# A transformer block on one core: exponentials seven steps behind instead of eight, the last steps in pairs of banks

## The chip, the cores and the metric

The kernel runs on one core of a Trainium2 chip. The metric is the device time of one execution in microseconds (us). The core has five engines with a queue each: PE (TensorE, matmuls), DVE (VectorE), ACT (ScalarE), POOL (GpSimd) and SP (which issues the DMAs). Each engine works through its own queue in order and waits there for semaphores. Matmuls write to PSUM, which has eight banks of 128 x 512 float32; SBUF holds the rest.

## The reference

The input is one sequence of 2048 tokens with 512 features in bfloat16. The block has 32 heads of 16 features and a feed-forward part with 1792 hidden features.

```python
def _A_ref(x, wqkv, wo):                 # H = 32, Dh = 16
    qkv = (x @ wqkv).reshape(B, S, 3, H, Dh).transpose(2, 0, 3, 1, 4)
    q, k, v = qkv[0], qkv[1], qkv[2]
    p = softmax(einsum("bhqd,bhkd->bhqk", q, k) * Dh ** -0.5)
    o = einsum("bhqk,bhkd->bhqd", p, v)
    return o.transpose(0, 2, 1, 3).reshape(B, S, D) @ wo

def _B_ref(x, w_gate, w_up, w_down):
    return (gelu(x @ w_gate) * (x @ w_up)) @ w_down

h = x + _A_ref(layernorm(x), A_wqkv, A_wo)
out = h + _B_ref(layernorm(h), B_w_gate, B_w_up, B_w_down)
```

## The kernel before

**The work and its order.** Attention is cut into 64 units: eight groups of 256 query tokens (`gi`, the last is `GL` = 7) times eight slots of four heads (`slot`). Each unit takes 16 steps of one Python loop, the tick; a tick's instructions are put into the engines' queues one after the other when the program is built. The scores of a unit are computed twice. The first pass (P1, line 797 on PE) writes a pair of score tiles to two PSUM banks and DVE takes the row maximum over both (line 806). One such maximum is a tick of the loop; there are 1024. After a unit's last tick `negm_pre` (lines 832 to 840 on POOL) makes the negated maximum, `negm_post` turns it with a DMA transpose into `STG`, and four ticks later (`ADDX`) POOL adds it into the queries (line 851). The second pass (P2, line 867 on PE) then gives the scores less their maximum, transposed, and ACT takes the exponential of each bank of 128 x 512 (line 879) into a ring of 34 tiles: 23 in `PTM`, 4 in `PTE`, 7 in `PTG`. P2 runs `LAGX` = 8 ticks behind the end of its unit's P1 (`P2_START = 16 + LAGX`), two tiles a tick. So a tick of the main loop holds one maximum and two exponentials, and when P1 is over, 24 ticks of P2 alone remain.

**The dense stream.** All other PE work runs beside this as items, one piece a tick, from two lists, `prio` and `ready` (class `Dense`): the projections, `item_pv` (probabilities times values, line 893, five ticks for a unit), `item_ofin` (turning its result, line 919), `item_oproj`, and for each group the feed-forward part: seven steps `f` of `item_gate` and `item_up` (line 1072) and two `item_down` (line 1122, residual at 1127). An item of `ready` starts only if `startable` allows it and if it is over before the next item of `prio` is due. Before the change both `item_down` of group 6 (`GL - 1`) are held back until the loop is over (`force`) and serve as filler then. Results leave PSUM through `evac_act`: on ACT, and on DVE once P1 is over (`dve_free`). Where a tick's items have too little for PE, `dummy` adds matmuls (line 1285); in the ticks after P1 a pair of ticks is filled to `FILL_2`.

**POOL.** POOL's smaller chains (`PoolStream`) are a first-in-first-out list, emitted against a budget of 1.19 us a tick: the gelu of a feed-forward step (lines 1062, 1063, 1064, then tanh on ACT at line 1055, then 1060, 1061 and the product at 1114), and the end of `item_ofin`: the inverse of the row sums (`inv`, line 928) and the product (`mul`, line 932). An entry that costs over 2 us, which is `inv` alone, isn't emitted in ticks 1, 2, 3, 13, 14 and 15 of each 16.

**The end.** `tail_a` and `tail_a2` project three quarters of the last group's attention output inside the loop, into banks 0 and 1 (lines 1153, 1164, 1168). After the last `item_pv`, `tail_b` does the last slot (`tail_norm`, line 1192; `tail_onT`, 1205; projection, 1237), the layer norm (1240 to 1251, with one POOL operation at 1249), the transposes of the result (`tail_hnT`, lines 1213, 1218, 1220) and the last group's feed-forward part. Between the steps of this serial chain `fill(n)` puts `n` units of dense work or dummy matmuls on PE.

Of the kernel before, what the change touches and what calls it, by code (L numbers as in the profile page):

```python
# [223 lines left out]
LAGX = 8  # L224
PAUSE = 1
DOUBLES = 20
FILL_2 = 4
FILL_LN = 16
# [5 lines left out]
def bass_sequential_preLN__mha_block__geglu_ffn__prompt_kernel(nc, A_x, A_wqkv, A_wo, B_x, B_w_gate, B_w_up, B_w_down, out):  # L234
    dbg = None
    with ExitStack() as es:
# [264 lines left out]
        def startable(it, room):  # L501
            if it[0] is item_gate and par_busy[it[1][1] % 2] and room < 10:
                return False
            if it[0] is item_down and it[1][0] == GL - 1 and not force[0]:
                return False
            if it[0] is item_down and it[1][1] == 0 and not force[0]:
                return not gut_left.get(it[1][0], 0) and dense.now >= gut_last.get(it[1][0], 0) + 1
            return it[0] is not item_projT or not (qks_busy.get(("a", qk_n[0] % 4)) or qks_busy.get(("b", qk_n[0] % 2)))

        class Dense:  # L510
# [17 lines left out]
            def _start(self, item):  # L528
                genfn, a, est, nb = item
                if self.single:  # L530
# [5 lines left out]
            def piece(self):  # L536
                if self.single and self.pause > 0:
                    return 0
                while True:
# [11 lines left out]
                    try:  # L551
# [11 lines left out]
                        if self.single:  # L563
                            banks.give(self.bank)
                            self.pause = PAUSE
# [28 lines left out]
        class PoolStream:  # L594
# [11 lines left out]
            def run(self, flush=False):  # L606
                while self.q and (flush or self.budget >= min(self.q[0][0], 1.0)):
                    if not flush and self.q[0][0] > 2.0 and dense.now % 16 in (1, 2, 3, 13, 14, 15):
                        break
# [8 lines left out]
        ticking = [False]  # L618
        pool = PoolStream()
# [158 lines left out]
        for fn_ in qk_late:  # L778
            fn_()
        early = {0: [lambda: stats_dve(12), c2_rest], 1: [lambda: stats_dve(13), lambda: stats_dve(14), lambda: stats_act(15)], 2: [c2_dve, c3_rest],  # L780
                 5: [c3_act], 9: [lambda: w_order("q", 1, "act")], 11: [lambda: w_order("k", 1, "act")], 16: [lambda: w_order("q", 2, "act")],
                 18: [lambda: w_order("k", 2, "act")], 20: [lambda: w_order("q", 3, "act")], 22: [lambda: w_order("k", 3, "act")]}
# [59 lines left out]
        def negm_post(ui):  # L842
# [5 lines left out]
            q_ap = QT[:, c, slot, 256 * hf:256 * hf + 256]  # L848
            def add():
                pool.spend(0.7)  # L850
# [9 lines left out]
        def p2_tile(ui, j, gp, jj):  # L860
# [3 lines left out]
            m, g, b = j // 2, 2 * gp + jj, banks.take()  # L864
# [5 lines left out]
            return (b, m, g)  # L870

# [173 lines left out]
        def gelu_chain(par, dE):  # L1045
# [4 lines left out]
            def later(n):  # L1050
                if not force[0] and act_lag[0] > LAG_OP + 0.1 * n:
# [14 lines left out]
        def gate_up_mms(b, gi, f, w, nm):  # L1066
            hT = hnT_l[gi % 2]
            hr = [("hnT", gi % 2, k) for k in range(2)]
# [78 lines left out]
        def tail_a(b):  # L1147
# [9 lines left out]
            dense.add(tail_a2, front=True, est=4, not_before=dense.now + 2)  # L1157
            return 1

        def tail_a2(b):  # L1160
            gp = GL % 2
            for k in range(2):
                for hc in range(3):
                    P.op("pe", lambda e, k=k, hc=hc: e.matmul(pbank[:, k, :], OnT[:, k, hc, :], wo_sb[:, hc, :], start=(hc == 0), stop=False),
                         reads=[("OHa", 0), "wo"], writes=[("pb", k)], sig=False)
                    if hc == 1:
                        yield 2
                P.op("pe", lambda e, k=k: e.matmul(pbank[:, k, :], ident[:], g_h(GL, k), start=False, stop=False),
                     reads=["ident", ("h", gp, k)], writes=[("pb", k)], sig=(k == 1))
                if k == 0:  # L1170
                    yield 2
            a_done[0] = True
            return 2
        a_done = [False]
# [34 lines left out]
        def tail_hnT(b, k):  # L1209
            gp = GL % 2  # L1210
            pt = pbank[:, b, :].bitcast(BF16)
            for dc in range(4):
                P.op("pe", lambda e, dc=dc: e.transpose(out=pt[:, 128 * dc:128 * dc + 128], in_=hn_sb[:, k, 128 * dc:128 * dc + 128], identity=ident[:]),
                     reads=[("OH", k), "ident"], writes=[("pb", b)], sig=(dc == 3))
            o_ap = hnT_l[gp][:, :, 128 * k:128 * k + 128]
            i_ap = pt[:, 0:512].rearrange("p (c s) -> p c s", c=4)
            if k == 1:
                P.op("act", lambda e: e.activation(out=o_ap, in_=i_ap, func=ACT.Copy), reads=[("pb", b)], writes=[("hnT", gp, k)])
            else:
                P.op("dve", lambda e: e.tensor_copy(out=o_ap, in_=i_ap), reads=[("pb", b)], writes=[("hnT", gp, k)])  # L1220
# [6 lines left out]
        def tail_b():  # L1227
            P.op("act", lambda e: e.activation(out=htmp[:, 0:1], in_=nhalf[:, 0:1], func=ACT.Gelu_apprx_tanh), reads=["nhalf"], writes=[("htmp", 0)])
            fill(3)
            while not a_done[0]:  # L1230
                fill(1)
            in_bank(tail_norm)
            fill(3)
# [20 lines left out]
            for k in (0, 1):  # L1254
                in_bank(tail_hnT, k)
            fill(2)
# [6 lines left out]
            for k in range(2):  # L1263
                down_h(k, GL, k)
# [28 lines left out]
        while True:  # L1293
# [5 lines left out]
            if tick == P2_START - 4:  # L1299
# [23 lines left out]
            elif p2_ok and tick % 2 == 0:  # L1323
                if tick == 16 * NU:
                    for b_ in (2, 3):
                        banks.give(b_)
                for d_ in (0, 1):
                    for jj in (0, 1):
                        t2l.append(p2_tile((t2 + d_) // 16, (t2 + d_) % 16, 1 - (tick + d_) % 2, jj))
                        p2_consume((t2 + d_) // 16, t2l)  # L1330
                        t2l = []
# [75 lines left out]
```

## Time and profile before

| | |
|---|---|
| median of 3 runs | 1243.05 us (1242.91 to 1243.18) |
| the profiled execution's own time | 1243.15 us |
| its span, first to last instruction | 1241.4 us |
| granted TensorE clock, mean | 0.997 |
| DVE busy | 1189.8 us (96%), of it 1162.4 us in line 806 |
| ACT busy | 1199.9 us (97%) |
| PE busy | 1137.8 us (92%) |
| POOL busy | 764.3 us (62%) |

The span leaves out 1.75 us of the execution's time. Busy times are sums over the whole span; the last maximum of P1 ends at 1184.9 us, so the 56.5 us behind it have another limit than the loop ahead of it, and the shares of the whole say little about them. An ACT instruction's duration covers its latency; back to back, instructions overlap, so the distance from start to start is its price in a queue. Times in this document are us from the span's start unless said otherwise.

### The profile page before, as it was taken

The numbers are of one execution on the slowest core, as the hardware profiler recorded it, in microseconds if no ns is written. First come the engines' busy times: TensorE is split into PE (matmuls) and PEld (weight loads), VectorE is DVE, ScalarE is ACT, GpSimd is POOL, SyncE is SP. The second block draws the span as 40 slices with busy tenths as digits, with TensorE's granted clock in tenths as the row PEclk, the third lists the DMA queues.
The fourth block names the chain that finished last, engine by engine and source line by source line (L and its number), as shares of the span: only waits on it lengthen the run. The fifth ranks groups of instructions, "written<-read, shape, count | busy, mean of one in ns | idle before, by whom it ended". The sixth has DMA issues, their size and how long they took to land.

```text
span 1241.4 us, 31438 instructions
## 1 busy us (share of the span) xinstructions
PE 1137.8 (92%) x12680; PEld 437.8 (35%) x12680; DVE 1189.8 (96%) x1088; ACT 1199.9 (97%) x2464; POOL 764.3 (62%) x1540
## 2 busy tenths in 40 slices
PE   7999888899999999999999998999999999999998
PEld 3333222233333333333333333333333333333335
DVE  8999999999999999999999999999999999999923
ACT  7899999999999999999999999999999999999992
POOL 8647774467746765376645777367654766547760
PEclk9999999999999999999999999999999999999989
DMA  5101004300010000100010000100002000100000
GB/s 151 31 22 28 24 19 130 89 6 3 6 31 12 6 6 6 38 5 6 4 27 18 4 6 6 27 17 6 6 4 40 6 4 6 27 19 3 6 13 18
DMA packets 50800, 27.45 MB, mean 22 GB/s; under 512 B 36064, under 2 KB 49632, under 8 KB 50656
## 3 DMA queue, kind: packets, MB, share of 16 engines
q1 hardware_dynamic: 50656, 25.45, 8.0%
q8 instruction: 101, 1.65, 0.5%
q14 instruction: 43, 0.35, 0.1%
HBM read 11.80 MB, written 2.10 MB: 11 GB/s over the span
## 4 chain that ended last, share of the span: by engine, by line
DVE 58%; ACT 30%; PE 9%; POOL 2%; issue 1%; DMA 0%
DVE PM L806 57%; ACT PTM L879 17%; ACT PTG L879 5%; ACT PTE L879 3%; PE pbank L1122 2%; PE pbank L867 2%; PE pbank L797 1%; ACT th_sb L1055 1%; PE pbank L1072 1%; ACT g_sb L641 1%; ACT OnT L1012 1%; ACT u_sb L641 1%; PE pbank L739 1%; PE pbank L998 1%; PE pbank L676 1%
## 5 line engine op out<-in xcount | busy, mean ns | idle before, releaser
L806 DVE TENSOR_REDUCE PM<-pbank 128x2 f32<-128x1024 f32 x1024 | 1162.4, 1224 | 5.3 <-PE pbank L867 2.8
L879 ACT ACTIVATE PTM<-pbank 128x512 bf16<-128x512 f32 x1388 | 737.0, 669 | 4.7
L867 PE MATMUL pbank<-QT,KT 32*128 32x256 bf16 x4096 | 498.2, 273 | 9.7 <-ACT PTM L879 4.4
L797 PE MATMUL pbank<-KT,QT 32*128 32x512 bf16 x2048 | 394.2, 382 | 46.4 <-DVE PM L806 23.6
L1285 PE MATMUL pbank<-ones_bf,ident 128*128 128x512 bf16 x794 | 245.3, 384 | 28.1 <-ACT PTM L879 3.2
L797 PEld LDWEIGHTS pbank<-KT,QT 32*128 32x128 bf16 x2048 | 104.5, 91 | 392.7 <-DVE PM L806 170.3
L879 ACT ACTIVATE PTG<-pbank 128x512 bf16<-128x512 f32 x420 | 228.2, 660 | 1.1 <-PE pbank L867 0.3
L867 PEld LDWEIGHTS pbank<-QT,KT 32*128 32x128 bf16 x4096 | 164.5, 92 | 65.7 <-ACT PTM L879 36.8
L879 ACT ACTIVATE PTE<-pbank 128x512 bf16<-128x512 f32 x240 | 137.7, 667 | 1.9 <-PE pbank L867 1.1
L893 PE MATMUL pbank<-PTM,VA 128*17 128x256 bf16 x2776 | 125.8, 274 | 2.7 <-ACT PTM L879 1.2
L832 POOL TENSOR_TENSOR MX<-PM,MX 128x8 f32<-128x8 f32 x64 | 12.9, 202 | 163.9 <-DVE PM L806 163.9
L1285 PEld LDWEIGHTS pbank<-ones_bf,ident 128*128 128x128 bf16 x794 | 47.6, 97 | 131.4 <-ACT PTM L879 83.8
L928 POOL TENSOR_TENSOR LINV<-OAT,negone 128x16 f32<-128x16 f32 (+1 forms) x32 | 92.7, 2896 | 0.0
L893 PEld LDWEIGHTS pbank<-PTM,VA 128*17 128x17 bf16 x2776 | 60.1, 89 | 46.9 <-issue 29.1
L821 POOL TENSOR_TENSOR MX<-PM,MX 128x8 f32<-128x8 f32 x64 | 13.0, 203 | 101.5 <-DVE PM L806 101.5
L1072 PE MATMUL pbank<-hnT_l,wu_sb 128*128 128x256 bf16 x448 | 67.1, 276 | 3.1 <-ACT PTM L879 0.2
L1072 PE MATMUL pbank<-hnT_l,wg_sb 128*128 128x256 bf16 x448 | 66.9, 275 | 2.5
L1114 POOL TENSOR_TENSOR GUT<-th_sb,u_sb 128x512 bf16<-128x512 f32 x49 | 62.2, 1270 | 5.1 <-DVE u_sb L630 3.0
L1061 POOL TENSOR_TENSOR th_sb<-th_sb,g_sb 128x512 f32<-128x512 f32 x49 | 62.1, 1268 | 4.1
L1064 POOL TENSOR_TENSOR th_sb<-th_sb,g_sb 128x512 f32<-128x512 f32 x49 | 62.1, 1268 | 3.1
L1062 POOL TENSOR_TENSOR th_sb<-g_sb 128x512 f32<-128x512 f32 x49 | 51.0, 1041 | 18.8 <-ACT g_sb L641 18.8
L1122 PE MATMUL pbank<-wd_sb,GUT 128*128 128x512 bf16 x224 | 60.5, 382 | 0.6 <-ACT PTM L879 0.2
(149 smaller groups left out, 1077.3 us busy)
## 6 DMA issues: line engine op xcount, KB each, us to landing
QKS<-QKS SPq DMA_DIRECT2D x27, 112.0 KB, 2.2
x_sb<-in_A_x_dram SPq DMA_DIRECT2D x4, 512.0 KB, 5.6
xres<-in_A_x_dram SPq DMA_DIRECT2D x16, 128.0 KB, 2.2
out_dram<-out_sb SPq DMA_DIRECT2D x16, 128.0 KB, 1.8
wg_sb<-in_B_w_gate_dram SPq DMA_DIRECT2D x4, 448.0 KB, 5.0
wu_sb<-in_B_w_up_dram SPq DMA_DIRECT2D x4, 448.0 KB, 4.0
wd_sb<-in_B_w_down_dram SPq DMA_DIRECT2D x3, 512.0 KB, 6.4
STG<-ST SPq DMA_TRANSPOSE x64, 2.3
```

The costliest lines, as they stand in the source:

```text
L797: P.op("pe", lambda e, g=g, b=b: e.matmul(pbank[:, b, :], QT[32 * g:32 * g + 32, c, slot, 128 * qt:128 * qt + 128], KT[32 * g:32 * g + 32, ...
L806: P.op("dve", lambda e: e.tensor_reduce(out=PM[:, par, qt, kc, g:g + 2], in_=pbank[:, b:b + 2, :], axis=AX.X, op=ALU.max), reads=[("pb", b ...
L867: P.op("pe", lambda e, kt=kt, i=i: e.matmul(pbank[:, b, 256 * i:256 * i + 256], KT[32 * g:32 * g + 32, slot, 128 * kt:128 * kt + 128], QT[ ...
L879: P.op("act", lambda e, b=b, pi=pi: e.activation(out=PTt(pi), in_=pbank[:, b, :], func=ACT.Exp), reads=[("pb", b)], writes=[("PT", pi)], e ...
L893: P.op("pe", lambda e, g=g, kt=kt, pi=pi, i=i: e.matmul(pbank[32 * g:32 * g + 17, b, 0:256], VA[:, kt, 4 * slot + g, :], PTt(pi)[:, 256 * ...
L928: P.op("pool", lambda e: e.tensor_tensor(out=li, in0=oat4[:, :, :, 16], in1=negone[:, 0:8 * ns].rearrange("p (q h) -> p q h", q=2), op=ALU ...
L1061: o(1.27, lambda e: e.tensor_tensor(out=ts_, in0=ts_, in1=gs, op=ALU.mult), [("th", par), ("g", par)])], then=done)
L1064: o(1.27, lambda e: e.tensor_tensor(out=ts_, in0=ts_, in1=gs, op=ALU.mult), [("th", par), ("g", par)])], then=lambda: defer(TANH_LAG, lamb ...
L1072: P.op("pe", lambda e, dc=dc, fc=fc, i=i: e.matmul(pbank[:, b, 256 * i:256 * i + 256], w[:, dc, 128 * fc:128 * fc + 128], hT[:, dc, :], st ...
L1114: P.op("pool", lambda e: e.tensor_tensor(out=o_ap, in0=shp(ts_), in1=shp(us), op=ALU.mult), reads=[("th", par), ("u", par)], writes=o_keys ...
L1122: P.op("pe", lambda e: e.matmul(pbank[:, b, :], GUT[:, fc, 128 * k:128 * k + 128], wd_sb[:, fc, :], start=first, stop=last), reads=[("GUT" ...
L1285: P.op("pe", lambda e: e.matmul(pbank[:, b, :], ident[:], ones_bf[:, 0:512], start=True, stop=True), reads=["ident", "ones_bf"], writes=[( ...
```

## The change

- `LAGX` goes from 8 to 7: P2 runs one tick nearer behind P1, so 23 ticks are left after P1. The loop's switch to one dense item at a time stays at tick 20 (`DOUBLES`), and four reorderings of weights on ACT (`w_order`) move from ticks 16 to 22 to ticks 13 to 19.
- In the ticks after P1 the two tiles of a tick lie in two neighbouring banks, and one ACT instruction takes the exponential of both (`p2_pair`, 128 x 1024); where the two ring tiles aren't neighbours in one tensor, it stays two instructions. Three pairs of banks go round, and the dense stream has the fourth.
- `item_down` of group 6, first half, may start inside the loop; only the second half is held back. `FILL_2` is 5 instead of 4.
- The tanh of a gelu waits while a gate or up item is under way (for up to 20 ticks), and its limit on ACT's planned backlog grows more slowly with the wait.
- `mul` isn't emitted in ticks 1 and 2 of a unit while the addition of line 851 is due. A dense item that ends after P1 is followed by no pause.
- `tail_a2` is no dense item any more: its two halves stand in `tail_b`, ahead of and behind `tail_norm`, in place of `fill(3)`. `FILL_LN` goes from 16 to 13. The last transposes get three banks of their own, the second half's copy is split between ACT and DVE, the `fill(2)` behind them is gone, and `down_h` of the last group comes ahead of the rest of the dense stream. `tail_b` begins with `dve_free` set back, so a dense item's result leaves through ACT there, no longer through DVE.

```diff
 ADDX = 4
-LAGX = 8
+LAGX = 7
...
 DOUBLES = 20
-FILL_2 = 4
-FILL_LN = 16
+FILL_2 = 5
+FILL_LN = 13
...
                 return False
-            if it[0] is item_down and it[1][0] == GL - 1 and not force[0]:
+            if it[0] is item_down and it[1] == (GL - 1, 1) and not force[0]:
...
                 genfn, a, est, nb = item
+                self.cur = genfn
...
                             banks.give(self.bank)
-                            self.pause = PAUSE
+                            self.pause = 0 if dve_free[0] else PAUSE
...
                 while self.q and (flush or self.budget >= min(self.q[0][0], 1.0)):
+                    if not flush and add_due[0] and qkv_over[0] and self.q[0][1].__name__ == 'mul' and dense.now % 16 in (1, 2):
+                        break
...
         ticking = [False]
+        add_due = [False]
...
         early = {0: [lambda: stats_dve(12), c2_rest], 1: [lambda: stats_dve(13), lambda: stats_dve(14), lambda: stats_act(15)], 2: [c2_dve, c3_rest],
-                 5: [c3_act], 9: [lambda: w_order("q", 1, "act")], 11: [lambda: w_order("k", 1, "act")], 16: [lambda: w_order("q", 2, "act")],
-                 18: [lambda: w_order("k", 2, "act")], 20: [lambda: w_order("q", 3, "act")], 22: [lambda: w_order("k", 3, "act")]}
+                 5: [c3_act], 9: [lambda: w_order("q", 1, "act")], 11: [lambda: w_order("k", 1, "act")], 13: [lambda: w_order("q", 2, "act")],
+                 15: [lambda: w_order("k", 2, "act")], 17: [lambda: w_order("q", 3, "act")], 19: [lambda: w_order("k", 3, "act")]}
...
             q_ap = QT[:, c, slot, 256 * hf:256 * hf + 256]
+            add_due[0] = True
             def add():
+                add_due[0] = False
...
 
-        def p2_tile(ui, j, gp, jj):
+        def p2_tile(ui, j, gp, jj, bank=None):
...
             assert ui in q_ready
-            m, g, b = j // 2, 2 * gp + jj, banks.take()
+            m, g, b = j // 2, 2 * gp + jj, banks.take() if bank is None else bank
...
             return (b, m, g)
+
+        def p2_pair(ui, tiles):
+            pis = []
+            for (b, m, g) in tiles:
+                pi = pt_n[0] % NPT; pt_n[0] += 1
+                assert pi not in pt_busy, "PT ring too small"
+                pt_busy.add(pi)
+                pt_of[(ui, m, g)] = pi
+                pis.append(pi)
+            (b0, b1), (q0, q1) = [t[0] for t in tiles], pis
+            assert b1 == b0 + 1
+            if q1 == q0 + 1 and pt_tiles[q0][0] is pt_tiles[q1][0]:
+                o_ap = pt_tiles[q0][0][:, pt_tiles[q0][1]:pt_tiles[q0][1] + 2, :]
+                P.op("act", lambda e: e.activation(out=o_ap, in_=pbank[:, b0:b0 + 2, :], func=ACT.Exp), reads=[("pb", b0), ("pb", b1)], writes=[("PT", q0), ("PT", q1)])
+            else:
+                for b, pi in ((b0, q0), (b1, q1)):
+                    P.op("act", lambda e, b=b, pi=pi: e.activation(out=PTt(pi), in_=pbank[:, b, :], func=ACT.Exp), reads=[("pb", b)], writes=[("PT", pi)])
...
             def later(n):
-                if not force[0] and act_lag[0] > LAG_OP + 0.1 * n:
+                if not force[0] and (act_lag[0] > LAG_OP + 0.04 * n or (n < 20 and dense.gen is not None and dense.cur in (item_gate, item_up))):
...
             hT = hnT_l[gi % 2]
-            hr = [("hnT", gi % 2, k) for k in range(2)]
+            hr = [("hnT", gi % 2, k) for k in range(2)] if gi != GL else [("hnT", gi % 2, 0), ("hnTx", 0), ("hnTx", 2)]
...
             P.op("dve", lambda e: e.tensor_copy(out=OnT[:, :, 0:3, :], in_=pt[:, 0:768].rearrange("p (k c s) -> p k c s", k=2, c=3)), reads=[("pb", b)], writes=[("OHa", 0), ("OH", 0), ("OH", 1)])
-            dense.add(tail_a2, front=True, est=4, not_before=dense.now + 2)
+            a_done[0] = True
             return 1
-
-        def tail_a2(b):
+        a_done = [False]
+
+        def tail_a2(k):
             gp = GL % 2
-            for k in range(2):
-                for hc in range(3):
-                    P.op("pe", lambda e, k=k, hc=hc: e.matmul(pbank[:, k, :], OnT[:, k, hc, :], wo_sb[:, hc, :], start=(hc == 0), stop=False),
-                         reads=[("OHa", 0), "wo"], writes=[("pb", k)], sig=False)
-                    if hc == 1:
-                        yield 2
-                P.op("pe", lambda e, k=k: e.matmul(pbank[:, k, :], ident[:], g_h(GL, k), start=False, stop=False),
-                     reads=["ident", ("h", gp, k)], writes=[("pb", k)], sig=(k == 1))
-                if k == 0:
-                    yield 2
-            a_done[0] = True
-            return 2
-        a_done = [False]
+            for hc in range(3):
+                P.op("pe", lambda e, hc=hc: e.matmul(pbank[:, k, :], OnT[:, k, hc, :], wo_sb[:, hc, :], start=(hc == 0), stop=False),
+                     reads=[("OHa", 0), "wo"], writes=[("pb", k)], sig=False)
+            P.op("pe", lambda e: e.matmul(pbank[:, k, :], ident[:], g_h(GL, k), start=False, stop=False),
+                 reads=["ident", ("h", gp, k)], writes=[("pb", k)], sig=False)
...
 
-        def tail_hnT(b, k):
+        def tail_hnT(b, k, dcs, eng):
...
             pt = pbank[:, b, :].bitcast(BF16)
-            for dc in range(4):
-                P.op("pe", lambda e, dc=dc: e.transpose(out=pt[:, 128 * dc:128 * dc + 128], in_=hn_sb[:, k, 128 * dc:128 * dc + 128], identity=ident[:]),
-                     reads=[("OH", k), "ident"], writes=[("pb", b)], sig=(dc == 3))
-            o_ap = hnT_l[gp][:, :, 128 * k:128 * k + 128]
-            i_ap = pt[:, 0:512].rearrange("p (c s) -> p c s", c=4)
-            if k == 1:
-                P.op("act", lambda e: e.activation(out=o_ap, in_=i_ap, func=ACT.Copy), reads=[("pb", b)], writes=[("hnT", gp, k)])
+            n = len(dcs)
+            for i, dc in enumerate(dcs):
+                P.op("pe", lambda e, i=i, dc=dc: e.transpose(out=pt[:, 128 * i:128 * i + 128], in_=hn_sb[:, k, 128 * dc:128 * dc + 128], identity=ident[:]),
+                     reads=[("OH", k), "ident"], writes=[("pb", b)], sig=(i == n - 1))
+            o_ap = hnT_l[gp][:, dcs[0]:dcs[0] + n, 128 * k:128 * k + 128]
+            i_ap = pt[:, 0:128 * n].rearrange("p (c s) -> p c s", c=n)
+            keys = [("hnT", gp, k)] if n == 4 else [("hnT", gp, k), ("hnTx", dcs[0])]
+            if eng == "act":
+                P.op("act", lambda e: e.activation(out=o_ap, in_=i_ap, func=ACT.Copy), reads=[("pb", b)], writes=keys[-1:])
             else:
-                P.op("dve", lambda e: e.tensor_copy(out=o_ap, in_=i_ap), reads=[("pb", b)], writes=[("hnT", gp, k)])
+                P.op("dve", lambda e: e.tensor_copy(out=o_ap, in_=i_ap), reads=[("pb", b)], writes=keys[-1:])
...
         def tail_b():
+            dve_free[0] = False
             P.op("act", lambda e: e.activation(out=htmp[:, 0:1], in_=nhalf[:, 0:1], func=ACT.Gelu_apprx_tanh), reads=["nhalf"], writes=[("htmp", 0)])
-            fill(3)
...
                 fill(1)
+            tail_a2(0)
             in_bank(tail_norm)
-            fill(3)
+            tail_a2(1)
...
             fill(FILL_LN)
-            for k in (0, 1):
-                in_bank(tail_hnT, k)
-            fill(2)
+            sp_ = [b for b in range(2, 8) if b not in (own, other)]
+            tail_hnT(sp_[0], 0, (0, 1, 2, 3), "dve")
+            tail_hnT(sp_[1], 1, (0, 1), "act")
+            tail_hnT(sp_[2], 1, (2, 3), "dve")
+            for k in range(2):
+                down_h(k, GL, k)
...
             NP = NFC // 2
-            for k in range(2):
-                down_h(k, GL, k)
...
                 break
-            if tick == P2_START - 4:
+            if tick == DOUBLES:
...
                 if tick == 16 * NU:
-                    for b_ in (2, 3):
-                        banks.give(b_)
-                for d_ in (0, 1):
-                    for jj in (0, 1):
-                        t2l.append(p2_tile((t2 + d_) // 16, (t2 + d_) % 16, 1 - (tick + d_) % 2, jj))
-                        p2_consume((t2 + d_) // 16, t2l)
-                        t2l = []
+                    own = dense.bank if dense.gen is not None else banks.free[0]
+                    other = own ^ 1
+                    banks.free = [other] if dense.gen is not None else [own, other]
+                    pairs = [0, 2, 10 - (own & 6)]
+                for d_ in ((0, 1) if t2 + 1 < 16 * NU else (0,)):
+                    b_ = pairs.pop(0)
+                    pairs.append(b_)
+                    ui_, j_ = (t2 + d_) // 16, (t2 + d_) % 16
+                    p2_pair(ui_, [p2_tile(ui_, j_, 1 - (tick + d_) % 2, jj, b_ + jj) for jj in (0, 1)])
...
```

## The prediction

> **What bounds the kernel now.** I read the page first, its chain of work and its costliest groups.
>
> ```profile
> DVE 58%; ACT 30%; PE 9%; POOL 2%; issue 1%; DMA 0%
> ...
> L806 DVE TENSOR_REDUCE PM<-pbank 128x2 f32<-128x1024 f32 x1024 | 1162.4, 1224 | 5.3 <-PE pbank L867 2.8
> L879 ACT ACTIVATE PTM<-pbank 128x512 bf16<-128x512 f32 x1388 | 737.0, 669 | 4.7
> ```
>
> The 1024 maxima bound the loop. In the timeline 18 of them take 20.45 us, so they start 1.131 apart ((20.45 - 1.23)/17). The first starts at 14.66, the last ends at 1184.92: 1170.3 us against 1024 x 1.131 = 1158. Of the 12 us between, about 5 lie before 33 us and some 6 in stretches where ACT is ahead in the chain, 0.9 us in each group of 128 ticks. So the loop has little to give. Behind it lie 56.5 us, and the table by stage and the chain show two parts.
>
> ```profile
> 1184.00:1199.00 15.00, 13.02 (x152) 5.74 (x150) 3.58 (x6) 14.81 (x31) 13.03 (x18) 1.00 0.08 24
> 1199.00:1206.00 7.00, 6.96 (x37) 2.09 (x37) 0.00 (x0) 5.60 (x12) 5.31 (x6) 0.52 0.00 0
> 1206.00:1212.00 6.00, 5.32 (x90) 2.53 (x89) 0.89 (x2) 5.98 (x12) 1.27 (x1) 0.99 0.01 3
> 1212.00:1220.00 8.00, 8.00 (x47) 3.83 (x46) 4.73 (x14) 2.61 (x5) 0.70 (x1) 1.00 0.05 17
> ```
>
> ```profile
> 1200.56 1.39 PE pbank L1164 x3
> 1201.95 0.43 PE pbank L1168
> 1202.38 0.56 PE pbank L867 x8
> 1202.94 1.39 PE pbank L1164 x3
> 1204.33 0.43 PE pbank L1168
> 1204.76 0.59 PE pbank L867 x8
> 1205.35 2.04 ACT PTG L879 x4
> 1207.39 3.93 ACT PTM L879 x8
> ```
>
> Columns of the table: PE, weight loads, DVE, ACT, POOL busy, then PE's clock. First part, to 1211.3: the 48 exponentials of the last 24 ticks, on ACT, which starts them at 1184.72. For some 7 us PE runs at 0.52 of its clock, `tail_a2` takes 0.43 us a matmul, and ACT waits for PE. Second part: the serial end.
>
> The timeline prices ACT's waits and the end:
>
> ```profile
> 1197.33 0.63 ACT L1055 ACTIVATE th_sb<-th_sb 128x512 f32<-128x512 f32 x1 [0.19 <-POOL th_sb L1064]
> 1202.95 0.60 ACT L879 ACTIVATE PTE<-pbank 128x512 bf16<-128x512 f32 x1 [1.10 <-PE pbank L867]
> 1207.25 4.06 ACT L879 ACTIVATE PTM<-pbank 128x512 bf16<-128x512 f32 x8
> 1217.14 0.74 DVE L1251 TENSOR_SCALAR OnT<-xres,mv,rstd 128x512 bf16<-128x512 bf16 x2 [0.88 <-POOL rstd L1249]
> 1218.44 0.61 PE L1213 MATMUL pbank<-ident,OnT 128*128 128x128 bf16 x8
> 1219.09 0.60 ACT L1218 ACTIVATE hnT_l<-pbank 128x512 bf16<-128x512 bf16 x1 [2.62 <-PE pbank L1213]
> 1219.97 1.04 PE L1072 MATMUL pbank<-hnT_l,wg_sb 128*128 128x256 bf16 x8
> ```
>
> Eight exponentials in 4.06 us with 0.72 for the last are 0.477 start to start: 48 x 0.477 = 22.9, two tanh at 0.52 are 1.0, and the remaining 2.7 of 26.6 us are ACT's waits, for tanh's input (0.6 beyond a back-to-back start), for PE (1.3 and 0.45) and small ones. In the end part the normalised rows are there at 1217.55 and 1217.88, but PE is in its fill until 1218.44.
>
> **The change part by part.** *One tick less.* Two exponentials (2 x 0.477 = 0.95) go from the tail into the loop. In the tail that is -0.95. In the loop ACT idles 0.94 us ahead of the evacuation at 44.67, where tick 23 lies, so it costs nothing there if that gap takes it, 0.95 if not.
>
> *Pairs.* The ring position at tick 1024 is 2002 mod 34 = 30; of the 23 pairs from there two straddle tensors (22/23 and 26/27), so 21 are one instruction and 4 exponentials stay single. An exponential over two banks isn't in this trace; the nearest row is a copy of 1024 elements from one bank:
>
> ```profile
> L487 ACT ACTIVATE xnT<-pbank 128x1024 bf16<-128x1024 bf16 x6 | 5.8, 1022 | 0.7 <-PE pbank L485 0.6
> ```
>
> Two of these take 1.94 us, 1.94 - 1.02 = 0.92 start to start, against 2 x 0.477 = 0.954: 0.04 saved a pair, 21 x 0.04 = -0.8. The bounds are 0.90 (an evacuation of 272 elements at 1181.98 is followed 0.28 us later, which with 0.477 for 512 makes 0.2 per 240) and 1.02 (no overlap at all, the row's own duration): -1.1 to +1.4. I take 0.915, as the operation is nearest in size. The Trainium skill (ScalarE: Activation LUTs, section "What ACT_TABLE_LOAD costs") gives 186 ns + 0.833 ns an element with 93 ns overlap, by which a pair would save 0.093 us and the sum be 1.1 us lower; the trace's 0.477 for 512 elements lies under that formula's 0.519, so I keep the rows.
>
> *What ACT waits for.* `tail_a2` leaves the loop, so no 0.43 us matmuls stand ahead of P2's tiles. To see the rest I followed the dense stream and POOL's list by hand through group 6. The step that decides is `inv` (line 928, 2.94 us). Now an odd unit's `item_ofin` ends in tick 13 of 16, where `inv` is barred, so it goes out in tick 0, behind the maximum's chain and ahead of the addition of line 851:
>
> ```profile
> L928 POOL TENSOR_TENSOR LINV<-OAT,negone 128x16 f32<-128x16 f32 x31 | 91.0, 2937 | 0.0
> L851 POOL TENSOR_TENSOR QT<-QT,STG 128x256 bf16<-128x256 bf16 x64 | 42.8, 668 | 19.6 <-DMA STG<-ST 19.4
> ```
>
> One tick earlier it ends in tick 12, where `inv` is allowed: 2.94 + 0.62 for `mul` run beside the last maxima and are over as the unit's last maximum ends. Then attention results come 4 ticks sooner, group 6's projection 2 ticks, and its last gate and up items fall at ticks 1021 to 1025 (now the last up stands at 1042). Its POOL chain is done near 1194, the first `item_down` fits ticks 1037 to 1041 and waits for nothing. ACT then has one tanh (0.52) in the tail, and waits for its input (POOL: chain to 1187.2, then 1.04, 0.62, 0.67, 1.27 makes 1190.9, against ACT there at 1190.2) about 0.6; between 0 and 1.5. PE needs per pair of ticks 8 P2 matmuls (0.5) and five or six units at 0.216 (1.1 to 1.3): 1.6 to 1.8 against ACT's 1.83.
>
> Sum: 1184.72 + 21 x 0.915 + 4 x 0.477 + 0.52 + 0.6 + 0.1 for the longer last one = 1207.05, against 1211.3: **-4.3**.
>
> *The end.* `tail_a2`'s halves are 4 matmuls (0.86) where three fill matmuls (0.65) stand. Ahead of `tail_norm` PE was free 0.27 us before the copy from DVE, here nearly covered; behind it PE was just in time: together **+0.3**. The fill ahead of the transposes shrinks from 18 matmuls, as they fell, to 12 and a dummy: 5 x 0.216 = 1.08, of which only what is late counts. The transposes then start at 1217.55 and 1217.9 with the rows; the copies, 0.42 on DVE, two halves after it on DVE and ACT, with ACT's evacuation of `item_down` (0.6 from 1217.6) ahead of its half, end at about 1218.6, and two `down_h` hide beside them. Gates start at 1218.65 instead of 1219.97: **-1.3**; were that evacuation late by its whole 0.6, -0.7.
>
> *The loop.* The addition must now be over one tick sooner. Over the units of the loop it ends at least 1.18 us ahead of P2's first matmul (unit 57), 1.76 in most odd units, 2.7 to 3.1 in most even ones; less a tick (1.09) that leaves 0.09, 0.67 and more, so nothing stalls even if `inv` stays where it is, and 3.5 us sooner is spare. Guarding `mul` takes 0.62 more out of its way. ACT's planned backlog peaks at 0.94 us twice a group in my count (now 0.84, where DVE loses 0.08 us): +0.15 each is +0.3 a group, +1.8 for six; the tanh rule spreads ACT's load elsewhere, and the 0.9 us a group lost now bounds the gain at -5, of which I credit 1.5. The four `w_order` leave ticks where P2 starts: 0 to +0.5. I take **+0.3** (-2 to +2.5). The pause costs and gains nothing: it is over by the next tick anyway.
>
> Total: -4.3 + 0.3 - 1.3 + 0.3 = -5.0 on 1243.15, the profiled execution's own time (span 1241.4 + 1.75), 0.1 above the median: **1238.1**.
>
> **The rivals.** *PE's clock halves again* (chance 0.12). It was 0.5 from 1199.3 to 1206.1, after a stretch in which PE waited for ACT. In such 6.8 us a pair of ticks costs PE 0.6 + 5.5 x 0.43 = 3.0 instead of 1.83, so some 2.3 pairs lose 1.15: +2.6, 1240.7. Against it: `FILL_2` is one more and the waits are gone; for it: waits of 0.4 us at each semaphore remain. The Trainium skill (TensorE: Matmul & The Clock Gate, Part 1) has about 3.4 us of idle time throttle PE; here it happened with no gap above 0.9 us, as its section "A second HAM failure mode: psum-queue depth-cycling", on short idles between groups, would have it.
>
> *The first `item_down` misses the loop* (0.10), if my hand count of ticks is off by four. Then 30 matmuls remain for a fill of 15 to 18, and 12 more (2.6 us) stand behind the transposes: 1240.7.
>
> *The addition comes late* (0.07; slower). If `inv` stays in tick 0 and one gelu operation (line 1062, 1.04 us) slips between it and the addition, an odd unit's P2 starts 1.04 - 0.67 = 0.37 us late; PE is in order, the next maximum's matmuls are behind it, and DVE has one pair ahead. 31 units give 11.5 us: 1249.6. It decides from an addition 0.9 us later than now, where 31 x 0.23 eats the gain. Against: after `inv` POOL's budget stands at -1.65, so nothing else went out before the addition.
>
> *The loop gains too* (0.08): if the new tanh rule removes half of the 0.9 us a group, -3: 1235.
>
> **How the numbers follow.** The forecast has 0.63, with 1236.5 to 1240 as its own range by the bounds above. The range 1235.5 to 1241.5 reaches to the two small rivals and leaves out the slow one. Within 0.2% is within 2.5 us of 1243.05, about what a measurement can tell; faster therefore means below 1240.55: 0.62 + 0.08 + 0.06 of the two rivals there = 0.76; same 0.15; slower 0.09.
>
> **What would show it.** Line 806 still ends near 1185; ACT's pairs start 0.9 apart, the last ends near 1207; no half clock behind 1185; `inv` ahead of the chain of lines 832 to 840; line 1122 in the loop's last ticks; gates 0.7 us behind the last row. Wrong: a wait of PE for line 851 each second unit, or P1 ending over 2.5 us later.

## The result, and the profile after

The changed kernel takes 1258.3 us in the median (1256.95 to 1258.68, 4 runs), the kernel before beside it 1243.12 (1242.91 to 1243.37): a ratio of 1.012, 95% interval 1.0103 to 1.0138. The forecast of 1238.1 was wrong, and in its sign: the change costs 15.2 us.

The profiled execution after took 1258.67, its span is 1256.9. First the page: the chain that ended last, then the groups for the maxima, the exponentials and POOL's addition (lines 806, 879 and 851 are now 810, 902 and 857).

```profile
DVE 38%; ACT 30%; POOL 13%; PE 12%; DMA 4%; issue 3%; POOLq 0%; DVEq 0%
...
L810 DVE TENSOR_REDUCE PM<-pbank 128x2 f32<-128x1024 f32 x1024 | 1167.3, 1214 | 20.1 <-PE pbank L873 17.1
L902 ACT ACTIVATE PTM<-pbank 128x512 bf16<-128x512 f32 x1357 | 730.5, 688 | 8.9 <-PE pbank L873 2.9
...
L857 POOL TENSOR_TENSOR QT<-QT,STG 128x256 bf16<-128x256 bf16 x64 | 42.7, 667 | 58.3 <-DMA STG<-ST 58.2
```

DVE has 38% of the chain where it had 58%. POOL has 13% (2% before) and DMA 4% (0%). The maxima now wait 20.1 us (5.3 before) and the addition 58.3 (19.6). The waits name the links between the two (us in total, times, longest):

```profile
POOL QT L857 <- DMA STG<-ST: 58.2, 42, 3.8
...
DVE PM L810 <- PE pbank L873: 17.1, 35, 2.8
...
ACT th_sb L1078 <- POOL th_sb L1087: 10.7, 20, 2.2
```

The last is the tanh of a gelu, waiting for POOL's third gelu product (1055 for 1064 before, where it was 1.4 us in 6 times).

**Where the time went.** The last maximum ends at 1204.87 instead of 1184.92, +20.0, of which the first one starts 0.4 later. Behind it 52.1 us remain instead of 56.5, -4.4. Together, unrounded, that is the +15.5 of the span. So the end came out nearly as forecast, and the loop lost time that no step of the prediction had in it.

To place the loss I take what each distance between starts of two maxima has above 1.1313 us (the prediction's 1.131 with one more digit). That sum is 11.7 us before and 31.3 after. By the tick's place in its unit of 16, from the second group of 128 ticks on: 7.6 us now stand at tick 6, 10.9 at tick 8 and 2.1 at tick 10; before, those three had 0.1, 0.1 and 0.7. The 10.9 are 0.23 behind each of 13 odd units (3.0 in all), 0.4 to 0.6 behind three (1.5), and three bursts of 1.26, 2.87 and 2.32 (6.4).

**One burst, followed through the queues.** POOL's timeline after, at an odd unit's end (start, duration, then idle time ahead and its releaser):

```profile
1014.16 2.93 POOL L951 TENSOR_TENSOR LINV<-OAT,negone 128x16 f32<-128x16 f32 x1
1017.17 0.62 POOL L955 TENSOR_TENSOR Otok<-OAT,LINV 128x256 bf16<-128x256 f32 x1
1017.75 0.20 POOL L836 TENSOR_TENSOR MX<-PM,MX 128x8 f32<-128x8 f32 x1
...
1019.50 0.23 POOL L844 TENSOR_TENSOR ST<-R,ST 128x8 bf16<-128x8 f32 x1
1019.66 1.04 POOL L1085 TENSOR_TENSOR th_sb<-g_sb 128x512 f32<-128x512 f32 x1
1020.78 0.62 POOL L1086 TENSOR_SCALAR th_sb<-th_sb 128x512 f32<-128x512 f32 x1
1023.75 0.67 POOL L857 TENSOR_TENSOR QT<-QT,STG 128x256 bf16<-128x256 bf16 x1 [2.34 <-DMA STG<-ST]
1024.37 1.26 POOL L1087 TENSOR_TENSOR th_sb<-th_sb,g_sb 128x512 f32<-128x512 f32 x1
```

And the same unit's chain and addition before:

```profile
1004.81 0.23 POOL L840 TENSOR_TENSOR ST<-R,ST 128x8 bf16<-128x8 f32 x1
1004.97 2.93 POOL L928 TENSOR_TENSOR LINV<-OAT,negone 128x16 f32<-128x16 f32 x1
1007.98 0.62 POOL L932 TENSOR_TENSOR Otok<-OAT,LINV 128x256 bf16<-128x256 f32 x1
1008.56 0.67 POOL L851 TENSOR_TENSOR QT<-QT,STG 128x256 bf16<-128x256 bf16 x1
1009.19 1.04 POOL L1062 TENSOR_TENSOR th_sb<-g_sb 128x512 f32<-128x512 f32 x1
```

Before, `inv` and `mul` fill the 3.5 us from the chain's end (1005.04) to the addition, and the DMA transpose of `STG` lands meanwhile. After, both lie ahead of the chain, as forecast. So two gelu operations come to stand behind the chain, 1.7 us in all, then the addition, which holds POOL until `STG` has landed, and the gelu's third operation (1087) waits behind it. In the odd units POOL's wait there was 0.7 us in all before; after, it is 0.7 to 0.9 us in 19 of the 32 and 2.3 to 3.8 in nine, 41 us in all. It costs DVE time where two gelu operations stand ahead of the addition and the third behind it: in units 11, 17, 25 and 33 it waits 2.4 to 3.8 us with no gelu operation ahead of it, and no loss at tick 8 follows.

What waits for 1087, on ACT, then PE and DVE:

```profile
1025.67 0.63 ACT L1078 ACTIVATE th_sb<-th_sb 128x512 f32<-128x512 f32 x1 [1.79 <-POOL th_sb L1087]
1026.20 2.04 ACT L902 ACTIVATE PTG<-pbank 128x512 bf16<-128x512 f32 x4
```

```profile
1026.84 0.39 PE L873 MATMUL pbank<-QT,KT 32*128 32x256 bf16 x2 [1.88 <-ACT PTG L902]
```

```profile
1028.78 1.23 DVE L810 TENSOR_REDUCE PM<-pbank 128x2 f32<-128x1024 f32 x1 [2.24 <-PE pbank L873]
```

The tanh was put into ACT's queue by the plan and holds the exponentials behind it, those hold PSUM banks, PE can't write the next P2 tile, and the maximum's matmuls stand behind that tile. Four queues in order pass on one late DMA. In this burst the addition starts 4.02 us behind the chain's end, where 0.23 is lost about 2.4; the last section comes back to the late ones.

**The end.** ACT after P1:

```profile
1204.63 2.08 ACT L890 ACTIVATE PTG<-pbank 128x1024 bf16<-128x1024 f32 x2
1206.91 3.77 ACT L890 ACTIVATE PTM<-pbank 128x1024 bf16<-128x1024 f32 x4 [0.20 <-PE pbank L873]
1211.42 0.63 ACT L1078 ACTIVATE th_sb<-th_sb 128x512 f32<-128x512 f32 x1 [0.74 <-POOL th_sb L1087]
1211.96 6.49 ACT L890 ACTIVATE PTM<-pbank 128x1024 bf16<-128x1024 f32 x7
```

Seven pairs and the step to the next instruction (1218.28) take 6.32 us: 0.903 a pair, start to start. The last exponential ends at 1227.75, the first gate of the tail starts at 1235.49: 7.74 us, where before it was 8.66. PE's clock is 1.00 from 1204 to 1236.

### The profile page after: what moved, and what is told of

Its sections match the earlier page's. It is cut to its first block, busy times and chain, and to the rows that moved or that the text cites. A ratio compares the mean times of both kernels' runs of the same rounds, so it can differ in the third digit from the quotient of the medians.

```text
span 1256.9 us, 31436 instructions
## 1 busy us (share of the span) xinstructions
PE 1141.7 (91%) x12683; PEld 438.0 (35%) x12683; DVE 1193.0 (95%) x1086; ACT 1203.1 (96%) x2446; POOL 762.5 (61%) x1540
## 4 chain that ended last, share of the span: by engine, by line
DVE 38%; ACT 30%; POOL 13%; PE 12%; DMA 4%; issue 3%; POOLq 0%; DVEq 0%
DVE PM L810 38%; ACT PTM L902 16%; ACT PTG L902 5%; POOL LINV L951 5%; DMA STG<-ST 4%; ACT PTE L902 3%; PE pbank L1145 3%; ACT th_sb L1078 2%; PE pbank L1305 2%; POOL th_sb L1087 2%; PE pbank L801 2%; PE pbank L873 2%; PE pbank L1095 1%; ACT g_sb L645 1%; ACT u_sb L645 1%
## 5 line engine op out<-in xcount | busy, mean ns | idle before, releaser
L810 DVE TENSOR_REDUCE PM<-pbank 128x2 f32<-128x1024 f32 x1024 | 1167.3, 1214 | 20.1 <-PE pbank L873 17.1
L873 PE MATMUL pbank<-QT,KT 32*128 32x256 bf16 x4096 | 508.5, 274 | 29.1 <-ACT PTM L902 15.7
L801 PEld LDWEIGHTS pbank<-KT,QT 32*128 32x128 bf16 x2048 | 100.5, 91 | 376.4 <-DVE PM L810 148.5
L873 PEld LDWEIGHTS pbank<-QT,KT 32*128 32x128 bf16 x4096 | 167.8, 92 | 90.1 <-ACT PTM L902 48.2
L825 POOL TENSOR_TENSOR MX<-PM,MX 128x8 f32<-128x8 f32 x64 | 12.9, 202 | 120.4 <-DVE PM L810 119.1
L857 POOL TENSOR_TENSOR QT<-QT,STG 128x256 bf16<-128x256 bf16 x64 | 42.7, 667 | 58.3 <-DMA STG<-ST 58.2
```

The lines of the kernel that those rows point to most:

```text
L801: P.op("pe", lambda e, g=g, b=b: e.matmul(pbank[:, b, :], QT[32 * g:32 * g + 32, c, slot, 128 * qt:128 * qt + 128], KT[32 * g:32 * g + 32, ...
L810: P.op("dve", lambda e: e.tensor_reduce(out=PM[:, par, qt, kc, g:g + 2], in_=pbank[:, b:b + 2, :], axis=AX.X, op=ALU.max), reads=[("pb", b ...
L873: P.op("pe", lambda e, kt=kt, i=i: e.matmul(pbank[:, b, 256 * i:256 * i + 256], KT[32 * g:32 * g + 32, slot, 128 * kt:128 * kt + 128], QT[ ...
```

## The experiments

My theory, called W in the expectations: the cost is the addition's wait in POOL's queue, passed on as above, because `inv` no longer stands between the chain and the addition. Beside it B: the feed-forward steps come sooner by the same moves and two of them bunch between two attention results, so that ACT's evacuations and tanh come too close together. The rivals: P2's nearness itself (`LAGX`; L), the new tanh rule (T), and the addition holding PE directly.

| kernel | median us | ratio, 95% interval | P1 ends | lost between maxima | last exponential ends | first gate of the tail |
|---|---|---|---|---|---|---|
| before (profile shown) | 1243.05 | | 1184.92 | 11.7 | 1211.31 | 1219.97 |
| after | 1258.3 | 1.012, 1.0103 to 1.0138 | 1204.87 | 31.3 | 1227.75 | 1235.49 |
| addx5 | 1243.9 | 1.0001, 0.9991 to 1.001 | 1190.25 | 16.8 | 1212.29 | 1220.03 |
| phase_kept | 1241.78 | 0.9984, 0.9974 to 0.9993 | 1184.50 | 11.0 | 1207.59 | 1217.82 |
| lag8 | 1242.4 | 0.9995, 0.9986 to 1.0004 | 1185.64 | 11.8 | 1209.66 | 1219.89 |
| tanh_old | 1257.08 | 1.0109, 1.0094 to 1.0124 | 1203.27 | 29.9 | 1226.15 | 1233.89 |
| tanh_tick7 | 1241.07 | 0.998, 0.9971 to 0.9989 | 1183.91 | 10.7 | 1206.44 | 1216.67 |
| mend | 1239.19 | 0.9966, 0.9954 to 0.9979 | 1184.62 | 11.5 | 1207.71 | 1216.14 |
| mend_single | 1239.17 | 0.9969, 0.9958 to 0.9981 | 1184.07 | 10.9 | 1207.78 | 1215.94 |
| mend_least | 1241.25 | 0.9982, 0.9973 to 0.999 | 1185.73 | 12.2 | 1209.13 | 1217.55 |

Each ratio is to runs of the kernel before on the same chip (medians 1243.68 beside addx5 to tanh_old, 1243.54 beside the rest). The last four columns are each from one profiled execution.

**addx5.** The changed kernel with the addition put into POOL's queue one tick later.

```diff
-ADDX = 4
+ADDX = 5
```

> The changed kernel with ADDX = 5: POOL's addition (line 857) is put into its queue one tick later, so that the gelu operation of line 1087 stands ahead of it and fills the time in which the addition waits for the DMA transpose. The order of all else is the same. Theory W (in the changed kernel the gelu operation stands behind the addition, the addition waits for its transpose, tanh on ACT waits for the gelu operation, and an ACT that has no time to spare passes that on to PE and DVE): ACT's waits for tanh's input fall from 10.7 us to under 2, DVE loses some 13 us less at tick 8 of the units, P1 ends near 1192 instead of 1204.9 and the time is 1244 to 1247. Rival L (P2 one tick nearer to the addition is what costs): the addition ends later still, so the time is 1258 or more. Theory B (bunched ACT work): stays at 1256 to 1258.

Measured 1243.9, just under what was expected: one number takes 14.4 of the 15.2 us away. The loss at tick 8 is gone (10.9 to 0.0), while tick 6 keeps 7.0 and tick 10 keeps 1.2. The groups:

```profile
L810 DVE TENSOR_REDUCE PM<-pbank 128x2 f32<-128x1024 f32 x1024 | 1163.4, 1212 | 9.4 <-PE pbank L873 7.4 <-PE pbank L801 1.6
...
L857 POOL TENSOR_TENSOR QT<-QT,STG 128x256 bf16<-128x256 bf16 x64 | 42.7, 667 | 37.3 <-DMA STG<-ST 37.3
...
L1078 ACT ACTIVATE th_sb<-th_sb 128x512 f32<-128x512 f32 x49 | 37.6, 767 | 0.0
```

ACT waits for no tanh any more (0.0; 10.7 after). The addition itself ends later than after, and PE now waits for it a few times (line 801 for 857: 2.3 us). So it is not P2 that the early addition hurt. In the first 128 ticks addx5 loses more than after (7.0 against 5.3; 5.5 before). Behind them after loses 26.0 us, addx5 9.8 and before 6.3, so of the loop's loss some 16 us are W's and 3.6 are what remains without it.

**phase_kept.** The changed kernel with attention results (`item_pv`) one tick later, which is where they were relative to P1 before, so that `inv` goes out in tick 0 again.

```diff
-                while not force[0] and dense.now < P2_START + 16 * ui + 4 * p + 5:
+                while not force[0] and dense.now < P2_START + 16 * ui + 4 * p + 6:
...
-                dense.add(item_pv, t2 // 16, front=True, est=5, not_before=tick + PV_T[0])
+                dense.add(item_pv, t2 // 16, front=True, est=5, not_before=tick + PV_T[0] + 1)
```

> The changed kernel, LAGX = 7, but item_pv starts and proceeds one tick later against P2, so that all dense items fall at the same ticks of P1 as before the change, inv in tick 0 again. Theories W and B both put the loss on where the dense items fall: DVE loses about 12 us in all as before, P1 ends at 1184 to 1186; the end then has both item_down as filler behind the loop, so it is 52 + 2.6 and the time 1240 to 1242. Rival L: P2 is still one tick nearer, odd units have 0.67 us less a transpose's bad days; P1 ends above 1195.

Both losses vanish (ticks 6 and 8 have 0.1 each), 11.0 us are lost in all, and P1 ends 0.4 sooner than before. `LAGX` = 7 is free in the loop once POOL's order is that of before. What is left of the gain is smaller than forecast since the first `item_down` now misses the loop: from the last exponential to the first gate it is 10.23 us, against 7.74 after (in lag8 and tanh_tick7 it is 10.23 too).

**lag8.** The change with `LAGX` back at 8.

```diff
-LAGX = 7
+LAGX = 8
```

> The changed kernel with LAGX = 8 and all else of the change kept (tanh rule, mul guard, w_order, pairs, tail). Theories W and B: dense items fall as before, P1 ends at 1184 to 1186, the end is 1 us longer than with LAGX 7 and has both item_down left: 1242 to 1244. Rival T (the new tanh rule costs): P1 ends above 1190.

11.8 us lost, and the end behind P1 is 55.7 us against 56.5. It undoes the move that brought `inv` to tick 12 together with the nearness of P2, so taken alone it doesn't tell W from the rival that P2's nearness is what costs; phase_kept does.

**tanh_old.** The change with the tanh rule of before.

```diff
-                if not force[0] and (act_lag[0] > LAG_OP + 0.04 * n or (n < 20 and dense.gen is not None and dense.cur in (item_gate, item_up))):
+                if not force[0] and act_lag[0] > LAG_OP + 0.1 * n:
```

> The changed kernel with the old rule for tanh's delay. Rival T (the new rule is what costs): P1 ends near 1185, the time is 1238 to 1240. Theories W and B: the feed-forward steps stand where they stand, tanh comes up to 2 ticks sooner, so it waits at least as long and the planned backlog peaks at 1.08 us instead of 0.96: 1258 to 1265.

1257.08, 29.9 us lost, ACT's wait for tanh input 9.8 us: the new rule is not the cause. Time and wait are a little under what was expected (1258 or more, and no less than 10.7). It only moves the smaller loss from tick 6 to tick 4 (7.1 us there).

**tanh_tick7.** This leaves the addition where it is and cuts the chain at its next link.

```diff
             def later(n):
+                if not force[0] and dense.now % 16 in (5, 6):
+                    defer(1, lambda: later(n))
+                    return
```

> The changed kernel, but the tanh of a gelu (L1078) isn't emitted in ticks 5 and 6 of a unit: what stood in tick 5 goes out in tick 7. inv stays in tick 12 for all 31 units and POOL's addition keeps its place and its wait for STG. Theory W (the late addition costs time only through the gelu operation behind it in POOL's queue, the tanh behind that and ACT's queue): the addition still waits some 55 to 60 us in all, but ACT waits for its tanh input under 2 us (10.7 with the change) and the maxima lose 12 to 17 us instead of 31.3; time 1240 to 1246. Rival (PE or DVE is held by the late addition itself, or by POOL's load): the maxima lose 25 us or more, time 1252 or more.

```profile
L810 DVE TENSOR_REDUCE PM<-pbank 128x2 f32<-128x1024 f32 x1024 | 1162.5, 1216 | 4.1 <-PE pbank L873 1.6 <-PE pbank L801 1.5
...
L857 POOL TENSOR_TENSOR QT<-QT,STG 128x256 bf16<-128x256 bf16 x64 | 42.7, 667 | 51.3 <-DMA STG<-ST 51.1
...
L1081 ACT ACTIVATE th_sb<-th_sb 128x512 f32<-128x512 f32 x49 | 35.3, 721 | 0.0
```

POOL waits 51.1 us for `STG`, somewhat less than after and than expected, and it costs nothing: 10.7 us are lost between the maxima, less than before and than expected, and the time is 1241.07. A busy or blocked POOL is not the cost; a tanh in ACT's queue ahead of its input is. This kernel also spreads the feed-forward steps (in the later groups the plan's count of ACT's backlog peaks at 0.84 us, as before, no longer at 0.96), so B's part is gone too. No run takes B away alone; its part is what addx5 keeps and this kernel and phase_kept do not. What B looks like is in ACT's timeline of after ahead of a tick 6:

```profile
1038.24 0.77 ACT L645 ACTIVATE g_sb<-pbank 128x512 f32<-128x512 f32 x1
1038.72 3.23 ACT L902 ACTIVATE PTM<-pbank 128x512 bf16<-128x512 f32 x6
1041.58 0.86 ACT L645 ACTIVATE u_sb<-pbank 128x512 f32<-128x512 f32 x1
1042.06 1.36 ACT L902 ACTIVATE PTM<-pbank 128x512 bf16<-128x512 f32 x2
1043.01 0.92 ACT L1078 ACTIVATE th_sb<-th_sb 128x512 f32<-128x512 f32 x1
```

No idle time stands in a bracket. A tick of 1.131 has two exponentials of 0.477, so 0.177 us to spare; two evacuations and a tanh are 0.48 + 0.48 + 0.52 = 1.48, which need over eight ticks and here come within eight exponentials, four ticks. The 0.77 that are missing reach DVE as a gap of 0.52 at tick 6 (1045.77), 14 times in the loop.

**mend.** phase_kept, and the last group's order made to fit again.

```diff
-                    dense.add(tail_a, front=True, est=3, not_before=max(dense.now + 5, 16 * NU))
+                    dense.add(tail_a, front=True, est=3, not_before=max(dense.now + 5, 16 * NU + 12))
...
-                dense.add(item_up, gi, f, est=3)
+                dense.add(item_up, gi, f, est=2 if gi == GL - 1 and f == 6 else 3)
...
-                dense.add(item_down, gi, k, est=5)
+                dense.add(item_down, gi, k, est=3 if gi == GL - 1 and k == 0 else 5)
...
-                yield 1
+            yield from ()
```

> Attention results one tick later, as in phase_kept (so inv stays in tick 0), and the last group's order made to fit: tail_a in one piece and not before 12 ticks after P1, the last up item with an estimate of 2 ticks and the first item_down with 3, so that the first half of item_down starts in tick 1042, inside the loop, and doesn't wait in the fill. Theory: P1 ends near 1184.5 as in phase_kept, and from the last exponential to the first gate it takes some 7.8 us as in the changed kernel, where phase_kept takes 10.2: P1's end plus 52 = span 1236.5 to 1237.5, time 1238 to 1239.5, 3 to 3.5 less than phase_kept's 1241.8. Rival (item_down waits for its gelu input ahead of PE's last P2 tiles and holds PE back): ACT's last exponential ends later than phase_kept's 1207.6 by 1 us or more, time 1240 to 1242.

1239.19, with mend_single the fastest here: 0.9966 of before. In the medians it is 2.6 us under phase_kept, the price that the prediction gave for an `item_down` that misses the loop; the traces show less, 1.7 in the spans. From the last exponential to the first gate it took 8.43 (10.23 in phase_kept), not 7.8: PE ends `item_pv` 1.1 us behind the last exponential, where it was 0.4 after, as the `item_down` stands ahead of it.

**mend_single.** mend, with each exponential of the last ticks an instruction of its own.

```diff
-            if q1 == q0 + 1 and pt_tiles[q0][0] is pt_tiles[q1][0]:
+            if False:
```

> mend, but every exponential of the last ticks is an instruction of its own over one bank. Theory (ACT bounds the last ticks; start to start 0.477 for one bank, 0.903 for two): 21 pairs at 0.051 more = 1.1 us later than mend. Rival (PE or the bank turnover bounds them): no difference, within 0.4 us of mend.

1239.17: no difference from mend in the medians. In the traces the tail's exponentials take 23.29 us with pairs (1184.42 to 1207.71) and 23.91 without. Of the 21 x 0.051 = 1.07 that the pairs save on ACT, 0.45 comes back as longer waits for PE and for tanh's input. From P1's end to the first gate it is 31.5 us with pairs and 31.9 without, less than these medians can tell. ACT is not alone in bounding the last ticks.

**mend_least.** mend with the old tanh rule, the old places of `w_order` and no guard on `mul`.

```diff
-                    if not flush and add_due[0] and qkv_over[0] and self.q[0][1].__name__ == 'mul' and dense.now % 16 in (1, 2):
-                        break
...
-                 5: [c3_act], 9: [lambda: w_order("q", 1, "act")], 11: [lambda: w_order("k", 1, "act")], 13: [lambda: w_order("q", 2, "act")],
-                 15: [lambda: w_order("k", 2, "act")], 17: [lambda: w_order("q", 3, "act")], 19: [lambda: w_order("k", 3, "act")]}
+                 5: [c3_act], 9: [lambda: w_order("q", 1, "act")], 11: [lambda: w_order("k", 1, "act")], 16: [lambda: w_order("q", 2, "act")],
+                 18: [lambda: w_order("k", 2, "act")], 20: [lambda: w_order("q", 3, "act")], 22: [lambda: w_order("k", 3, "act")]}
...
-                if not force[0] and (act_lag[0] > LAG_OP + 0.04 * n or (n < 20 and dense.gen is not None and dense.cur in (item_gate, item_up))):
+                if not force[0] and act_lag[0] > LAG_OP + 0.1 * n:
```

> mend with the old rule for tanh, the old places of the four w_order, and no guard on mul. Theory: these three parts are worth nothing in the loop once inv is in tick 0: P1's end and the time within 0.8 us of mend. Rival (the new tanh rule spreads ACT's load and gives the loop some of its gain): the maxima lose 1 us or more above mend.

A miss: 2.06 us over mend in the medians, 1.4 in the spans. P1 ends 1.1 later: the first maximum starts 0.3 later, 0.6 is lost in the first 128 ticks, where the four `w_order` lie, and 0.1 in each of the five groups from the third to the seventh; in the last group mend loses 0.4 more. The maxima lose 0.8 us more in all, so the rival's 1 us is not reached either. The three parts together do give something; which of the last two gives the 0.1 a group was not told apart.

## Why the prediction was wrong

- **The step that failed** is "nothing stalls even if `inv` stays where it is, and 3.5 us sooner is spare". It compared the addition with P2's first matmul alone. That comparison held in nearly every unit: in most odd ones after, the addition still ends 1.58 us ahead of P2's first matmul, and in the loop PE waits for it twice, 0.63 and 0.18 us, both in bursts. It left out what stands behind the addition in POOL's own queue, and that `inv` had been the work that covered the transpose's landing. The change was read as taking `inv` out of the addition's way; it took away the addition's cover. The prediction's own sum for the last unit has this order (1.04, 0.62, the addition's 0.67, 1.27 behind the chain) and no wait of the addition in it; there that wait was 0.72 us. addx5 (14.4 us from one tick) and tanh_tick7 (the wait kept, the cost gone) show it.
- **The slow rival** named the addition and the odd units, gave 1249.6 and had 0.07. Its condition was the wrong one, `inv` staying in tick 0 with P2 late behind the addition. The fault came with `inv` moved, and by way of tanh.
- **The peaks of ACT's planned backlog** were counted rightly (0.94 forecast, 0.96 in the plan) and priced at 0.15 each. They cost a gap of 0.52 at tick 6 and under 0.1 at tick 10, 8.5 us in 14 times, two a group in seven groups, of which the gaps of before that they replaced are to be taken off: with W gone, addx5 loses 3.6 us more than before behind the first 128 ticks. The loop term of +0.3 (-2 to +2.5) measured +20.0: some 16 us of it had no term in the sum, and these peaks were priced too low.
- **The last ticks**, forecast from the first exponential to the last as 22.33 us, took 23.1. The pairs were cheaper than the forecast 0.915 (0.903, 0.25 in all); the waits were 1.37 (0.47 for PE, 0.90 for tanh's input) against 0.6, and the last one ends 0.3 behind its slot, not 0.1. That the first `item_down` fits the loop, that no half clock comes there, and that the gate then starts 1.0 sooner behind the last exponential (0.9 measured) was right. The whole end gained 4.4 of the forecast 5.3.
- **That pairs are worth 0.8** was argued from ACT's queue alone. mend_single shows no difference in the time.
- **The rival that the clock halves again** has no support behind P1, where the clock of after and mend is 1.00 but for the last microsecond. The half clock came back inside the loop, behind a stall (below).

## What to carry to other kernels

Before an operation is taken out of the way of a waiting one on the same in-order queue, ask what the waiting one waits for: if it is a DMA, the operation was its cover, and the wait then falls on whatever is queued behind. Follow such a wait through each queue in turn (here POOL, ACT, PE, DVE), not only to the direct reader of the delayed data. And an operation that a plan puts into a full queue at a fixed time should keep slack to its input: two ticks for tanh, or one for the addition, were worth 14 to 17 us here.

## What was not expected of the hardware

One stall can bring the half clock with it. In after, around the longest gap of the loop (columns as in the prediction's table by stage):

```profile
614.00:616.00 2.00, 1.47 (x38) 0.72 (x30) 2.00 (x3) 0.97 (x2) 0.71 (x2) 1.00 0.00 0
616.00:618.00 2.00, 0.40 (x4) 0.14 (x4) 1.73 (x2) 0.80 (x2) 1.25 (x2) 0.98 0.00 0
618.00:620.00 2.00, 1.63 (x8) 0.38 (x10) 0.00 (x0) 1.78 (x4) 1.92 (x3) 0.50 0.00 0
...
622.00:624.00 2.00, 2.00 (x11) 0.48 (x11) 1.68 (x2) 1.49 (x3) 0.00 (x0) 0.50 0.00 0
624.00:626.00 2.00, 2.00 (x16) 0.42 (x15) 1.52 (x2) 1.38 (x4) 0.00 (x0) 0.81 0.00 0
```

PE idles 0.63 us (for the addition itself) and then 1.88, and from about 618 to 625 it runs at 0.50. At that clock a tick doesn't fit, and the next three maxima lose 0.38, 0.38 and 0.58 on top of the stall's 2.87. The same follows the gap of 1.88 at 1024.96, and one of 1.38 at 318.41, for 3.4 us each. These are the three bursts of tick 8. The Trainium skill (TensorE: Matmul & The Clock Gate, Part 1) puts the throttle behind about 3.4 us of idle time; the longest gap in this loop is 1.88, with a few matmuls before it, so the trace does not bear out that figure as a length of one gap.

The transpose of `STG` usually lands some 2.4 us after the chain's end, but took 3.3 to 4.5 in eight units of after, the three with the bursts among them. The DMA table of the one shown (1019 to 1024.5; queue, kind: packets, MB, share):

```profile
q1 hardware_dynamic: 288, 0.07, 6.3%
q8 instruction: 1, 0.02, 1.6%
q14 instruction: 1, 0.01, 0.4%
```

An instruction packet moves while the transpose is under way. Over the ten traces, of the additions that waited for `STG`, 80 started more than 2.65 us behind the chain's end, and in each of the 80 a packet of kind instruction started between 0.3 us ahead of the chain's end and 0.3 us ahead of the addition; of the 187 that started within 2.46 us, 10 had one. So late transposes go with instruction packets. That the packet holds the transpose up is not shown, since no run here moved one.
